# Reordering the rounding, the x sums and the direct sums in the second stage of a fused attention and leaky-ReLU feed-forward kernel

## The chip, the cores and the metric

The kernel runs on one core of a Trainium2 chip. The metric is the device time of one execution in microseconds (us). Engines go by the profile's names: PE multiplies matrices, PEld loads its weights, DVE is the vector engine, ACT the scalar engine, POOL is GpSimd, SP issues most of the transfers.

## The reference

```python
kv  = einsum('bhsd,bhse->bhde', k, v)          # 8 batches, 8 heads, 576 rows, 64 wide
out = einsum('bhsd,bhde->bhse', q, kv)
x   = out / sqrt(mean(out*out, -1) + 1e-6) * g_norm      # then (B,H,S,D) -> (4608, 512)
h   = x @ w_in                                 # 512 -> 2048
g   = maximum(0.01 * h, h)
y   = g @ w_out                                # 2048 -> 512, float32
```

`w_in` and `w_out` arrive in 64-bit floats and are rounded to 32-bit on the chip.

## The kernel before

**Stages.** The 4608 rows of x are cut into nine blocks of 512. Block 0 is multiplied directly while the weights are still arriving (`first_block`); the weights of the last quarter of the hidden width are not needed for it. After it come units of work, each one block by one quarter (chunk c) of the hidden width: block 1 with chunks 0 to 3 (units 0 to 3), block 0 with chunk 3 (unit 4), then blocks 2 to 8 with all chunks. Units 0 to 4 use one level of Strassen's seven products; from unit 5 on the first product uses two levels. This document calls units 0 to 4 the second stage.

**Slots.** A unit has seven slots, one for each product k of `ORDER = (1, 2, 6, 5, 7, 3, 4)`. The slot number is `at = 7 * now + t`, so unit 0 has slots 0 to 6, unit 1 slots 7 to 13, and so on to 34. A slot issues one product of h (eight matmuls into a bank named h_a to h_d) and, from slot 9 on, one product of the output of the unit before (into o_a or o_c): the o products run two slots behind. The bank of an h product has to be read by ACT or DVE before the product after the next can write it, and likewise o_a and o_c. In program order a slot then issues the postponed stores (`write_later`), the reads, a part of the rounding of a weight tile, the "direct" sums, and steps of the attention of block 2.

**Order.** `pin` keeps an instruction in program order. In the second stage all compute instructions are pinned, so each of PE, ACT, DVE, POOL and SP works through its own list, and an instruction that waits holds up what stands behind it. In `first_block` the sums made by `add` (L697) are not pinned.

**Rounding.** A tile's rounding (`round_f64`) has seven steps: two copies of its low and high words on ACT (L264, L262), a clamp on DVE (L266), an empty step, an activation on ACT (L271), and two instructions on DVE (L281, L284). There are 32 tiles. Tiles 0 to 23 are used by block 0; tile 22 and tile 23 are read by its last two output products. Tiles 24 to 31 are chunk 3. Tile j's raw words share a buffer with tile j + 2, so load j + 2 (`load_w`, SP) waits for tile j's two copies.

**x's sums.** `sides_x` makes the four sums of a block of x (DVE). For block 1 they are made near the end of `first_block`, by the letter x in `plan`.

**POOL.** L1198 is a copy of one element whose only purpose is a wait: POOL starts its sums behind it. Its list is then: `sides_w1(0)` and `more` (sums of the first weights, into `pairs`), `sides_w2` (also `pairs`), `combine(0, 0)`, and, slot by slot, the same for later chunks. At the end of every unit `sums_of` makes four sums gs1 to gs4 of g; output product 6 reads gs2, the third output product of the unit.

**combine and its homes.** `combine(c, part)` makes the second-level sums of chunk c into a home inside `stage` (six homes of 512 elements; a group of two products takes two homes, a group of one takes one), and postpones their store to a DRAM table. A home can be written again once the store has landed. Parts 0 and 1 come from `pairs`; part 2, the "direct" sums, comes from the weights themselves, in a first half (products 1 and 2) and a second half (product 4). Chunk 0's direct sums are on DVE, in slots 18 and 19 (first half), 22 and 23 (second half), both in home 2. The others are on POOL, by `DIRECT`.

```python
HOMES = {(0, 0): (2,), (0, 1): (4,), (1, 0): (0,), (1, 1): (2,), (2, 0): (4,), (2, 1): (0,),
         (3, 0): (4,), (3, 1): (0,), (0, 2): (2, 2), (1, 2): (2, 4), (2, 2): (0, 2), (3, 2): (4, 5)}
```

Of the kernel before, what the change touches and what calls it, by code (L numbers as in the profile page):

```python
# [24 lines left out]
def kernel(  # L25
# [36 lines left out]
    nc = tc.nc  # L62
# [29 lines left out]
    pin = tc.keep_in_program_order  # L92
    steady = first_done = in_line = in_first = in_block_1 = in_loop = False
# [13 lines left out]
    NW = U * NE * P  # L107
# [14 lines left out]
    def pair(i, *shape):  # L122
        return view(pairs, i * NW, *shape)
# [163 lines left out]
    w_jobs = []  # L287
# [7 lines left out]
    n0 = 4 * K * U  # L295
# [6 lines left out]
    def load_w(j, *eng):  # L302
        eng = eng or (nc.sync,)
        dst, src = w_jobs[j]
        if w_in.dtype == I64:
            w_raws[j] = load_f64(src.bitcast(U32), eng)
        else:
            load(dst, src, eng)

    def rounding(j, high_first=False):  # L310
        if w_in.dtype == I64:
            yield from round_f64(w_jobs[j][0], w_raws.pop(j), high_first)

    halfway = collections.deque()
# [15 lines left out]
    def finish_w():  # L330
        while halfway:
            for _ in halfway.popleft():
                pass
# [362 lines left out]

    def add(eng, out_, a, b_, minus=False, pinned=False):  # L697
        ins = eng.tensor_tensor(out_, a, b_, op=ALU.subtract if minus else ALU.add)  # L698
        if pinned or steady or in_block_1:
            pin(ins)  # L700

    def sides_w1(c):
# [16 lines left out]
    units = [(1, c) for c in range(NC)] + [(0, c) for c in range(K, NC)]  # L719
# [18 lines left out]
    def sides_w2(n):  # L738
# [7 lines left out]
        def sums(i):  # L746
# [15 lines left out]
            else:  # L762
# [13 lines left out]
    SLOT = {1: 0, 2: 1, 4: 2, 5: 3, 6: 4, 7: 5, 3: 6}  # L776
    w1_dram = [dram.tile([P, 7, 7, P], F32, name=f"w1_{c}") for c in range(NC)]
    HOMES = {(0, 0): (2,), (0, 1): (4,), (1, 0): (0,), (1, 1): (2,), (2, 0): (4,), (2, 1): (0,),
             (3, 0): (4,), (3, 1): (0,), (0, 2): (2, 2), (1, 2): (2, 4), (2, 2): (0, 2), (3, 2): (4, 5)}

    def combine(c, part, eng=None, only=(0, 1)):

# [315 lines left out]
                           pieces=pieces)  # L1098

    def go(steps, n=None):  # L1100
        while n is None or n > 0:
            if next(steps, steps) is steps:
                return
            n = None if n is None else n - 1
# [58 lines left out]
    t, a, f, x = "tafx"  # L1163
# [6 lines left out]
    loaded, x_sides = 12, None  # L1170
# [20 lines left out]
    in_first = True  # L1191
    first_block(between)
    in_first = False
    first_done = True
    rounded, rest = 26, collections.deque((3,))
    steps = halfway[0]
    in_block_1 = True
    pin(nc.gpsimd.tensor_copy(pair(0, NW)[:1, :1], x_sides[4][:1, 0, :1]))  # L1198
    h_sides, more = sides_w1(0)
    more()  # L1200
    sides_w2(0)[1](0)
    go(combine(0, 0))
    sides_w2(0)[1](1)
    in_loop = True

    LATE_ONE = {15: 2, 16: 2, 17: 1, 18: 1, 19: 2}
    A_SLOTS = {18: 1, 19: 2, 22: 1, 23: 1, 24: 2, 26: 1, 27: 1, 28: 2, 29: 2, 30: 1, 31: 1, 34: 2}
    DIRECT = {25: ((1, (0, 1)), (3, (1,))), 27: ((2, (0, 1)),), 29: ((3, (0,)),)}
    READS = {26: 2, 28: 4, 30: RING}
    PARTS = {33: ("11", "12"), 35: ("22",), 37: ("21",)}  # L1210

# [12 lines left out]
    def second_of(n):  # L1224
        if n in seconds:
            os_, finish = seconds.pop(n)
            return Second(n, os_["11"], finish)
# [7 lines left out]
    now, N1 = -1, NC + NC - K  # L1235
    rounds = [(1, range(NC)), (0, range(K, NC))] + [(i, range(NC)) for i in range(2, NB)]
    for i, chunks in rounds:
        one = in_block_1 = i < 2
        steady = not one
        if i == 1:  # L1240
            late, a_steps = a_steps, attention(2)
        elif i > 1:
            late, a_steps = a_steps, attention(i + 1, fine=True) if i + 1 < B else iter(())
        os = {}
        for c in chunks:
            now += 1
            nxt = units[now + 1] if now + 1 < len(units) else (NB, 0)
            g_sides = {}
            h_steps = product_h(now, h_sides, x_sides, g_sides) if one else \
                product_h_two(i, c, now, quarters, g_sides, second_of(now - 2))  # L1250
            for t in range(7):
                slot = 7 * c + t
                go(h_steps, 1)
                if not one:

                    if t == 6:
                        go(h_steps, 1)
                    if slot in LATE_SLOTS:
                        go(late, 1)
                    for _ in range(FINE_SLOTS.get(slot, 0)):  # L1260
                        go(a_steps, 1)
                    if i + 1 < NB:
                        if slot == 20:
                            x_sides, new_quarters, sums, inner = sides_x(i + 1)
                        if slot in (20, 21, 22):
                            go(sums, 2 if slot == 20 else 1)
                        if slot == 24:
                            inner(0)
                        elif slot == 25:
                            inner(1)  # L1270
                    load_some()

                if now - 1 in seconds:
                    for half in range(2):
                        if t == (6 if half else 4):
                            inner_g(now - 1, half)
                    if t == 5 and now - 1 < 2 * NC + NC - K:
                        inner_w2(units[now - 1][1])
                if (7 * now + t == 7 * NC + 4):
                    while writes:  # L1280
                        pin(nc.sync.dma_start(*writes.pop()))
                if slot in HELD and i == NB - 1:
                    pass
                elif waited == LAG:
                    go_o()
                elif o_queue:
                    waited += 1
                write_later()
                at = 7 * now + t
                for key in PARTS.get(at, ()):  # L1290
                    if at == 33:
                        part_os = os
                    load_part(part_os, key)
                if at in READS:
                    read(READS[at])
                if one:
                    if not rest and rounded < len(w_jobs):
                        finish_w()
                        steps = rounding(rounded)
                        rest.extend((3, 4) if rounded == 26 else (3, 3, 1))  # L1300
                        rounded += 1
                    if rest:
                        go(steps, rest.popleft())
                    if loaded < min(rounded + 2, len(w_jobs)):
                        load_w(loaded)
                        loaded += 1
                    for chunk, only in DIRECT.get(at, ()):
                        go(combine(chunk, 2, only=only))
                    if at == 18:
                        direct_0 = combine(0, 2, nc.vector)  # L1310
                    if at in (18, 19, 22, 23):
                        go(direct_0, 1)
                    if t == 3 and nxt[0] < 2 and nxt[1] != c:
                        h_sides, more_h = sides_w1(nxt[1])
                        if now == 0:
                            go(combine(0, 1))
                    if t == 5 and nxt[0] < 2 and nxt[1] != c:
                        more_h()
                    if t == 0 and units[now - 1][1] != c and now > 0:
                        for part in range(2):  # L1320
                            go(combine(c, part))
                    if at in (15, 16):
                        load_pair(2, at - 15)
                    go(late, LATE_ONE.get(at, 0))
                    go(a_steps, A_SLOTS.get(at, 0))
                    load_some(2 if at in (19, 20, 24, 25) else 1)
                    if at == 7 * NC - 4:
                        x_sides, _, sums, _ = sides_x(0)
                    elif at == 7 * N1 - 4:
                        x_sides, new_quarters, sums, inner = sides_x(2)  # L1330
                    if at in (7 * NC - 4, 7 * NC - 3, 7 * N1 - 4, 7 * N1 - 3):
                        go(sums, 2)
                    if at == 7 * N1 - 3:
                        inner(0)
                    elif at == 7 * N1 - 2:
                        inner(1)

            for _ in range(2 if i == NB - 1 and c == NC - 1 else 0):
                go(h_steps, 1)
                go_o()  # L1340
            go(h_steps)
            if c == NC - 1 and i != 1 and i + 1 < NB:
                inner(2)
                quarters = new_quarters
            by_two = NC + NC - K <= now < len(units) - 2
            if by_two:
                seconds[now] = (os, store(i))
            o_queue.append(product_o(now, g_sides, os, store(i), by_two))
# [32 lines left out]
```

## Time and profile before

| what | value |
|---|---|
| median of 3 runs (917.18 to 919.55) | 917.3 us |
| the profiled execution, its own time | 917.92 us |
| its span | 916.1 us |
| PE busy | 906.5 us (99%) |
| PEld, DVE, ACT, POOL busy | 783.6, 622.0, 346.9, 391.3 us |
| second stage, 112.9 to 228.5 us: busy of PE, DVE, ACT, POOL | 113.2, 78.1, 41.2, 101.0 us |
| granted clock of PE | 1.00 |
| transfers | 202.16 MB, mean 221 GB/s |

The profiled execution took 1.8 us more than its span, and 0.6 us more than the median. PE's share of busy time says that PE is nearly always at work; what it does not say is how tightly its products follow each other, since the end of a matmul is modelled. For that the starts are compared: eight matmuls of 128x256 start 1.73 us after the eight before them where nothing is late.

### The profile page before, as it was taken

What the parts mean: (1) busy time and instruction counts of PE and PEld (TensorE: products, weight loads), DVE (VectorE), ACT (ScalarE), POOL (GpSimd) and SP (SyncE); (2) the same over time, 40 slices, a digit from 0 to 9 for tenths busy, and PEclk for the clock granted to TensorE, in tenths of its full rate; (3) what the DMA queues carried; (4) which work ended last, traced back from release to release, by engine and by line L of the source; (5) the groups of instructions that cost most, each with busy time, mean ns of one, the idle gap of its engine ahead of it and who ended that gap; (6) DMA issues with size and microseconds to landing.
All of it is one profiled execution on the core that took longest, in us unless ns stands there. A gap on an engine that the chain in (4) does not pass through costs nothing.

```text
span 916.1 us, 18138 instructions
## 1 busy us (share of the span) xinstructions
PE 906.5 (99%) x7024; PEld 783.6 (86%) x7024; DVE 622.0 (68%) x1127; ACT 346.9 (38%) x679; POOL 391.3 (43%) x467
## 2 busy tenths in 40 slices
PE   8999999999999999999999999999999999999998
PEld 4544488878998999899999999999999999999997
DVE  5765865768657876587756786678659755755565
ACT  5756564221335233533343324332443333223330
POOL 2000499959633473226321642264226422642222
PEclk9999999999999999999999999999999999999999
DMA  8997185796998778876886789657765676667633
GB/s 257 256 249 198 55 274 170 234 325 199 348 329 264 228 212 267 234 228 217 249 264 218 220 249 272 222 174 230 223 183 178 188 221 198 181 189 225 195 111 93
DMA packets 92405, 202.16 MB, mean 221 GB/s; under 512 B 10016, under 2 KB 44448, under 8 KB 92320
## 3 DMA queue, kind: packets, MB, share of 16 engines
q1 hardware_dynamic: 81344, 189.14, 69.4%
q10 hardware_dynamic: 10528, 10.69, 3.4%
q8 instruction: 56, 0.92, 0.4%
q0 software_dynamic: 448, 1.18, 0.3%
q14 instruction: 29, 0.24, 0.1%
HBM read 173.44 MB, written 27.53 MB: 219 GB/s over the span
## 4 chain that ended last, share of the span: by engine, by line
PE 83%; DMA 6%; DVE 6%; ACT 3%; issue 1%; POOL 0%; SPq 0%; ACTq 0%; DVEq 0%; POOLq 0%
PE o_c L126 19%; PE o_a L126 19%; PE h_ha L126 11%; PE h_hb L126 11%; PE h_hc L126 8%; PE h_hd L126 8%; PE o_ps L126 3%; DMA pairs<-in_moe_w_out_dram 2%; PE h_b L126 1%; DMA stage<-in_moe_w_in_dram 1%; PE h_a L126 1%; DMA pairs<-in_v_dram 1%; PE h_c L126 1%; PE h_d L126 1%; DMA stage<-in_moe_w_out_dram 1%
## 5 line engine op out<-in xcount | busy, mean ns | idle before, releaser
L698 POOL TENSOR_TENSOR gs<-g 128x512 f32<-128x512 f32 x66 | 85.2, 1291 | 249.5 <-ACT g L913 249.5
L913 ACT ACTIVATE g<-g 128x512 f32<-128x512 f32 x127 | 80.1, 631 | 152.0 <-DVE g L698 150.1
L1032 ACT COPY w_all<-h_ha 128x512 f32<-128x512 f32 x84 | 48.9, 582 | 169.7 <-PE h_ha L126 159.6
L126 PE MATMUL o_a<-pairs,gs 128*128 128x256 f32 x392 | 93.1, 380 | 0.9 <-DVE o L698 0.9
L126 PE MATMUL o_c<-pairs,gs 128*128 128x256 f32 x392 | 93.3, 381 | 0.5 <-POOL gs L698 0.5
L698 DVE TENSOR_TENSOR o<-h_hb,o 128x128 f32<-128x128 f32 x104 | 29.9, 287 | 83.1 <-ACT pairs L1032 83.0
L126 PEld LDWEIGHTS o_c<-pairs,gs 128*128 128x128 f32 x392 | 71.3, 190 | 10.2 <-POOL pairs L698 1.2
L126 PEld LDWEIGHTS o_a<-pairs,gs 128*128 128x128 f32 x392 | 71.3, 190 | 9.2 <-issue 1.2
L698 DVE TENSOR_TENSOR o<-o_a,o 128x512 f32<-128x512 f32 (+1 forms) x93 | 62.6, 673 | 21.8 <-PE o_a L126 21.3
L698 DVE TENSOR_TENSOR o<-o_c,o 128x512 f32<-128x512 f32 x80 | 54.8, 684 | 26.4 <-PE o_c L126 26.2
L126 PE MATMUL h_ha<-stage,w_all 128*128 128x128 f32 x448 | 59.6, 276 | 0.0
L126 PEld LDWEIGHTS h_ha<-stage,w_all 128*128 128x128 f32 x448 | 56.6, 192 | 3.0 <-issue 0.7
L698 DVE TENSOR_TENSOR g<-g,pairs 128x512 f32<-128x512 f32 x84 | 55.7, 689 | 1.9
L698 POOL TENSOR_TENSOR pairs<-g 128x128 f32<-128x128 f32 x52 | 23.8, 457 | 77.2 <-PE h_hb L126 48.4
L698 DVE TENSOR_TENSOR w_all<-h_hc,w_all 128x512 f32<-128x512 f32 x56 | 38.4, 685 | 15.7 <-PE h_hc L126 15.6
L698 DVE TENSOR_TENSOR o<-h_hd,o 128x128 f32<-128x128 f32 x78 | 22.2, 285 | 38.1 <-ACT pairs L1032 38.0
L126 PE MATMUL h_hb<-stage,w_all 128*128 128x128 f32 x336 | 46.7, 275 | 0.0
L698 POOL TENSOR_TENSOR gs<-g,gs 128x512 f32<-128x512 f32 x33 | 45.5, 1380 | 0.0
L698 POOL TENSOR_TENSOR gs<-gs,g 128x512 f32<-128x512 f32 x33 | 44.1, 1335 | 2.6
L1032 ACT COPY pairs<-h_hb 128x384 f32<-128x384 f32 x84 | 40.0, 476 | 13.3 <-PE h_hb L126 12.6
L126 PE MATMUL o_acc<-w,g 128*128 128x512 f32 x96 | 43.7, 598 | 0.4 <-DVE w L284 0.3
L126 PE MATMUL h_ha<-xT,w_all 128*128 128x128 f32 x224 | 43.3, 275 | 0.2 <-ACT g L913 0.2
(240 smaller groups left out, 2242.3 us busy)
## 6 DMA issues: line engine op xcount, KB each, us to landing
w_all<-w SPq DMA_DIRECT2D x196, 448.0 KB, 4.2
pairs<-w SPq DMA_DIRECT2D x56, 512.0 KB, 4.4
out_dram<-o ACTq DMA_DIRECT2D x35, 256.0 KB, 5.2
v_in<-in_v_dram SPq DMA_DIRECT2D x27, 288.0 KB, 4.5
k_in<-in_k_dram SPq DMA_DIRECT2D x26, 288.0 KB, 4.1
q_in<-in_q_dram SPq DMA_DIRECT2D x52, 144.0 KB, 5.7
q_in<-in_q_dram SPq DMA_DIRECT2D x52, 140.0 KB, 5.7
w<-stage SPq DMA_DIRECT2D x12, 512.0 KB, 4.2
```

The source lines that it names most:

```text
L126: pin(nc.tensor.matmul(*args, **kw))
L698: ins = eng.tensor_tensor(out_, a, b_, op=ALU.subtract if minus else ALU.add)
L913: first_turn(nc.scalar.activation(t, t if src is None else src, func=AF.Prelu, alpha=SLOPE))
L1032: nc.scalar.copy(q[:, at], bank)
```

## The change

- `add` in `first_block` is pinned, so x's four sums for block 1 stand on DVE where the program has them: behind tile 22's rounding and ahead of tile 23's clamp.
- L1198, POOL's first instruction, reads tile 23's rounded weights in place of the last of x's sums.
- The rounding of tiles 25 to 31 follows a table. Its steps stay in their slots, but the two copies on ACT (and the load of the tile three ahead, on SP) are issued at the head of the slot, ahead of the slot's h product, where they were behind it.
- Chunk 0's second direct half goes from home 2 to home 5, and from slots 22 and 23 to slot 20 (both of its steps).
- Chunk 3's second direct half, in home 5, goes from POOL (slot 25) to DVE (slots 25 and 26).
- `combine(3, 0)` and `combine(3, 1)`, POOL, go from slot 21 to slot 22; their places in other units stay.

```diff
@@ def add
-        if pinned or steady or in_block_1:
+        if pinned or steady or in_first or in_block_1:
@@ HOMES
-             (3, 0): (4,), (3, 1): (0,), (0, 2): (2, 2), (1, 2): (2, 4), (2, 2): (0, 2), (3, 2): (4, 5)}
+             (3, 0): (4,), (3, 1): (0,), (0, 2): (2, 5), (1, 2): (2, 4), (2, 2): (0, 2), (3, 2): (4, 5)}
@@ after first_block
-    rounded, rest = 26, collections.deque((3,))
-    steps = halfway[0]
+    tiles = {25: halfway.popleft(), **{j: rounding(j) for j in range(26, len(w_jobs))}}
+    ROUND = {0: ((), ((25, 3),)), 1: (((26, 2),), ((25, 1), (26, 1))), 2: ((), ((26, 4),))}
+    for j in range(27, len(w_jobs)):
+        at = 3 * (j - 26)
+        ROUND.update({at: (((j, 2),), ((j, 1),)), at + 1: ((), ((j, 3),)), at + 2: ((), ((j, 1),))})
-    pin(nc.gpsimd.tensor_copy(pair(0, NW)[:1, :1], x_sides[4][:1, 0, :1]))
+    pin(nc.gpsimd.tensor_copy(pair(0, NW)[:1, :1], w_jobs[n0 - 1][0][:1, 0, :1]))
-    DIRECT = {25: ((1, (0, 1)), (3, (1,))), 27: ((2, (0, 1)),), 29: ((3, (0,)),)}
+    DIRECT = {25: ((1, (0, 1)),), 27: ((2, (0, 1)),), 29: ((3, (0,)),)}
@@ the slot, ahead of its h product
+                if one:
+                    for j, steps in ROUND.get(7 * now + t, ((), ()))[0]:
+                        go(tiles[j], steps)
+                        if loaded < min(j + 3, len(w_jobs)):
+                            load_w(loaded)
+                            loaded += 1
@@ the slot, behind it
-                    if not rest and rounded < len(w_jobs):
-                        finish_w()
-                        steps = rounding(rounded)
-                        rest.extend((3, 4) if rounded == 26 else (3, 3, 1))
-                        rounded += 1
-                    if rest:
-                        go(steps, rest.popleft())
-                    if loaded < min(rounded + 2, len(w_jobs)):
-                        load_w(loaded)
-                        loaded += 1
+                    for j, steps in ROUND.get(at, ((), ()))[1]:
+                        go(tiles[j], steps)
...
-                    if at == 18:
-                        direct_0 = combine(0, 2, nc.vector)
-                    if at in (18, 19, 22, 23):
-                        go(direct_0, 1)
+                    if at in (18, 25):
+                        direct = combine(*((0, 2, nc.vector) if at == 18 else (3, 2, nc.vector, (1,))))
+                    go(direct if at >= 18 else (), {18: 1, 19: 1, 20: 2, 25: 1, 26: 1}.get(at, 0))
...
-                    if t == 0 and units[now - 1][1] != c and now > 0:
+                    if t == now // 3 and units[now - 1][1] != c and now > 0:
                         for part in range(2):
                             go(combine(c, part))
```

More of the change, by code (lines that the diff above doesn't have):

```diff
@@ L1100, in go @@
     def go(steps, n=None):
+        steps = iter(steps)
         while n is None or n > 0:
```

## Prediction

> **What bounds the kernel.** The page first: PE is busy 99% of the span, so the time falls only by what PE waits, and rises by any new wait. Next, the view of waits for PE alone: engine and product, what released it, us in total, times, longest.
>
> ```profile
> PE o_a L126 <- DVE o L698: 0.9, 1, 0.9
> PE o_c L126 <- POOL gs L698: 0.5, 1, 0.5
> PE h_b L126 <- ACT g L938: 0.4, 1, 0.4
> PE h_a L126 <- issue: 0.3, 1, 0.3
> PE o_acc L126 <- DVE w L284: 0.3, 1, 0.3
> ```
>
> All five lie between 105 and 219 us; after 235 us the timeline of PE shows none. Modelled ends hide part of each, so I take starts from PE's timeline (start, duration):
>
> ```profile
> 105.42 3.67 PE L126 MATMUL o_acc<-w,g 128*128 128x512 f32 x8
> 109.38 3.67 PE L126 MATMUL o_acc<-w,g 128*128 128x512 f32 x8 [0.29 <-DVE w L284]
> ...
> 118.07 1.93 PE L126 MATMUL h_c<-xt,pairs 128*128 128x256 f32 x8
> 120.33 1.97 PE L126 MATMUL h_a<-xT,pairs 128*128 128x256 f32 x8 [0.33 <-issue]
> ...
> 188.77 1.99 PE L126 MATMUL h_b<-xT,pairs 128*128 128x256 f32 x8
> 191.64 1.97 PE L126 MATMUL o_a<-pairs,gs 128*128 128x256 f32 x8 [0.88 <-DVE o L698]
> ```
>
> Against 3.43 us (512 columns) and 1.73 us (256), the losses are: A, before the last two o_acc products, 0.28 + 0.53 = 0.8 us (tiles 22 and 23 late); B, slots 3 to 9, 0.53 + 0.07 + 0.21 + 0.10 + 0.58 + 0.07 = 1.5 us (ACT late at h's banks); C, slot 25, 2.87 − 1.83 (the usual step behind a kv group) + 0.07 = 1.1 us; D, slot 32 (2.35 − 1.73 + 0.10) and before slot 35 (0.3), 1.0 us. **Sum 4.4 us**, the most that can be won.
>
> C's cause is on DVE: chunk 0's second half waits for home 2's store, and the add that frees o_a stands behind it:
>
> ```profile
> 187.19 1.34 DVE L698 TENSOR_TENSOR stage<-w_all 128x128 f32<-128x128 f32 x1 [5.73 <-DMA w<-stage]
> 188.56 1.24 DVE L698 TENSOR_TENSOR stage<-stage,w_all 128x128 f32<-128x128 f32 x1
> ...
> 190.82 0.68 DVE L698 TENSOR_TENSOR o<-o_a,o 128x512 f32<-128x512 f32 x1
> ```
>
> **What the Trainium skill says.** "SBUF — State Buffer", SBUF: two separate sides, says that GpSimd and DVE share one port pair, an exclusive lock for a whole instruction, taken also by a DVE instruction with two SBUF inputs. The trace agrees: the two DVE adds above of 1.34 and 1.24 us overlap POOL sums, the same adds at 191.42 and 191.61, with POOL idle, take 0.26 and 0.27. "Perfetto Trace Analysis", Identifying the Most-Contended Engine, says that matmul busy time is a poor measure; the losses above, twice the waits listed, agree. "DMA: Bandwidth & Descriptors", Anatomy of one DMA, puts most of a transfer's fixed cost into the receipt of the last byte, so a home is free well after its store is issued: here the two stage stores at 187.35 take 3.4 and 4.4 us to land.
>
> **Part 1, x's sums and the gate.** Before, the sums fill DVE's gaps within tile 22 (starts 100.27 to 103.98). Behind it, from the same rows: the last multiply at 100.27 (1.0 us to the next start), clamp 101.27, L281 1.12 us after the clamp, L284 0.60 later, 102.99; four sums at 0.60: 103.60 to 106.0; tile 23's clamp 106.0, L281 107.12, L284 107.72, end 108.41. Tile 22 ends at 103.7 for 105.27: A's first loss goes. Tile 23 ends at 108.4 for 109.23, for POOL no longer runs beside it. The relu ahead of the last product then decides: it is 1.67 us behind L271 in ACT's list (105.64 to 107.31), so 108.12 to 108.7. A gains 0.8 − 0.2 = 0.6.
>
> The price is POOL's start. Its gate, now at 104.89, comes at 108.6: **3.8 us later**, with everything behind it. This is the list before:
>
> ```profile
> 104.89 0.75 POOL L1198 COPY pairs<-xt 1x1 f32<-1x1 f32 x1 [98.50 <-DVE xt L698]
> ...
> 123.02 1.53 POOL L698 TENSOR_TENSOR pairs<-w_all 128x512 f32<-128x512 f32 x1 [1.23 <-DMA w<-pairs]
> ...
> 134.62 1.28 POOL L698 TENSOR_TENSOR gs<-gs,g 128x512 f32<-128x512 f32 x1
> ```
>
> gs2 ends at 135.90; PE's third o product, slot 11, reads it at 138.65: 2.65 us of slack with 0.1 of latency. The wait of 1.23 us at 123.02 (a store of `pairs`) vanishes in the lateness, leaving 2.6. Contention may add 0.3 (the rounding now runs wholly beside POOL) or take up to 1.1 (tile 23 and the clamp of 24 are past). I take 2.2, ends 1.5 and 2.9. SP's store at 121.81 waits for POOL too, and load 29 (122.98) and the next `pairs` stores (125.72) wait behind it. I price that at nothing: load 29 is issued about 126, lands in 3 to 5 us, and slot 9's ACT then still has some 3 us before slot 11 needs its bank.
>
> **Part 2, copies at the head.** In slots 1, 3, 6, 9, 12 and 15 two ACT copies (start to start 0.57, 1.15 us a pair) go ahead of the bank's reader. In slot 1 they fall into ACT's wait of 1.90 us before 117.98, so slot 2's copy starts at its product's end and the 0.53 goes; clamp 27 comes earlier, which pulls slot 4's and 5's adds and the relus forward, and slot 7's copy ends about 0.3 us before slot 9 needs it. B's 1.5 us goes, counted alone; low end 0.9, should clamp and relus stay late.
>
> **A and B together** let PE reach slot 11 by 0.6 + 1.5 = 2.1 us earlier, but gs2 allows only 2.65 − 2.2 = **0.45** (−0.25 to 1.15). The rest becomes a wait on POOL at slot 11.
>
> **Part 3, direct sums.** Chunk 0's second half at slot 20 needs home 5, last stored in slot 17: free. Its four adds run beside POOL's 512-wide sums, up to 1.3 us each, from 176.9 to at most 182; the o_a add behind them must be done by 181.8. Cost 0 to 0.9, I take 0.4. C yields 1.1 − 0.4 = 0.7.
>
> Chunk 3's second half, now on DVE in slot 25, writes home 5 again. `combine(3, 0)` filled homes 4 and 5, now in slot 22 behind two 512-wide sums (2.5 us): POOL finishes it at 184.25 + 2.5 + 2.2 = 189. Its store belongs to slot 25 of SP, behind chunk 0's three stores, four `pairs` stores, one more, and six loads; at 0.5 to 0.8 us an issue after 183.8 that is about 191.7. It lands 3.4 us on, 195.1. DVE reaches the add at 192.8, so **DVE waits 2.3 us for a stage store once more**. Behind it on DVE stand two of x's sums and slot 26's h_d add; behind that add on ACT stand the relu and the four reads of o_ps (198.31 to 200.64, 2.33 us); behind those PE's next o_ps group, in slot 27:
>
> ```profile
> 201.45 0.88 PE L126 MATMUL o_ps<-qT,kv 64*32 64x384 f32 x16
> ```
>
> Landing + 0.4 + 2.3 (two short adds and two sums beside POOL) + 0.72 (add to relu) + 2.33 + 0.1 = landing + 5.9 = 201.0. PE would be there, with A to C won, at 201.45 − 1.15 = 200.3. So 0.7 us of the 1.15 goes back: **0.45 left** at slot 27 (from −1.0, landing at 196.5, to 1.15).
>
> POOL loses four 128-wide sums (1.8 us), and its wait of 11.15 us at 200.81, which stood on chunk 0's second half, ends. gs2 of unit 3 comes about 207 for 218.46: D's 0.7 goes; x's sums at 219 to 226 us, 1.2 to 1.8 us each beside POOL, fall back towards 0.6, so the 0.3 before slot 35 goes too. **D gains 1.0.**
>
> **Sum.** 0.45 + 1.0 = 1.45, taken as **1.5 us** (0 to 2.8 from the ends above). The profiled span of 916.1 us becomes 914.6, its execution 917.92 becomes 916.4; against the median, 0.6 us below that execution, 917.3 becomes 915.8. Beyond 235 us PE has no wait to absorb anything.
>
> **The rivals.**
> - *All gaps close.* POOL beside less DVE work is only 1.5 us late or less, and home 5's store lands by 194. For it: PE had 2.65 us of slack at slot 11. Against it: the 3.8 us. Won 3.7 to 4.4, so 913.3. Chance 0.17.
> - *Slower: home 5's store is late.* SP reached slot 25's stores only at 194.4 to 196.3 before. If it is as late again, the landing is about 199.7, PE's o_ps group starts at 205.6, 4.2 later than before, less D's 1.0: 920.5. Each us of landing counts fully; the result is slower than before from a landing at 196.6 and beyond the bound from 199.3. Against it: SP then stood behind a q load that waited for the DVE transpose at 189.73, itself behind the stall that goes. Chance 0.15.
> - *Slower, by the output's store.* SP's store at 219.38 had waited 11.0 us, put down to out_dram, a transfer that ACT issues in slot 31. If in the new order that wait falls ahead of the home 2 store of slot 27, POOL's next direct half and gs2 of unit 3 come behind it, at about 224: PE waits some 8 us in slot 32, 924. Chance 0.07.
> - *No effect.* The sums' order and the gate change little and the DVE wait only moves from slot 22 to 25: 917.3. Chance 0.05.
>
> **How the numbers follow.** About 0.3% (2.75 us) is what a measurement can tell from no change. The forecast has 0.56: nearly all of it inside, 0.03 beyond on the fast side. Faster: 0.17 + 0.03 = 0.20. Slower: 0.15 + 0.07 = 0.22. Same: 0.53 + 0.05 = 0.58. The forecast's own range is 914.5 to 917.3; the range goes to 913.4 (all gaps closed, nearly) and to 921.0 (home 5 late), leaving out the out_dram case and the ends.
>
> **What would show it.** POOL's L1198 at 108 to 109 us; the o_acc products 3.4 and 3.4 to 3.7 apart; no ACT wait of PE in slots 4 and 9, but one on POOL gs (or `pairs`) by slot 11, at 137.5 to 139; no DVE wait at 181 to 187, but one of 1 to 4 us on w<-stage near 193; o_ps in slot 27 near 201; no POOL wait of PE at slot 32. It is wrong if slot 11 starts before 137 (POOL kept up), if the DVE wait is absent, or if PE waits anywhere after 230 us.

## The result, and the profile after

The changed kernel takes **921.74 us** (median of 10, 920.84 to 922.99) beside 917.59 us for the kernel before (10 runs, 916.77 to 921.07). The ratio is 1.0040, 95% interval 1.0029 to 1.0052: slower, where 915.8 had been forecast. The profiled execution has a span of 919.3 us (916.1 before) and took 921.13 us, 0.6 us under its median.

The waits of PE come first again (engine and product, what released it, us in total, times, longest):

```profile
PE o_ps L126 <- ACT xT L421: 3.2, 1, 3.2
...
PE h_a L126 <- DVE g L698: 0.6, 1, 0.6
PE h_c L126 <- POOL stage L698: 0.6, 1, 0.6
...
PE h_b L126 <- ACT g L938: 0.3, 1, 0.3
PE o_acc L126 <- ACT g L1144: 0.3, 1, 0.3
```

The waits of o_a on DVE (0.9) and of o_c on POOL (0.5) are gone. In their place stands one of 3.2 us that before did not have, and two of 0.6 at h's banks. PE's timeline after (start, duration) shows where:

```profile
104.77 3.60 PE L126 MATMUL o_acc<-w,g 128*128 128x512 f32 x8
108.66 3.70 PE L126 MATMUL o_acc<-w,g 128*128 128x512 f32 x8 [0.29 <-ACT g L1144]
...
117.42 1.99 PE L126 MATMUL h_c<-xt,pairs 128*128 128x256 f32 x8
119.25 1.89 PE L126 MATMUL h_a<-xT,pairs 128*128 128x256 f32 x8
121.73 1.97 PE L126 MATMUL h_c<-xT,pairs 128*128 128x256 f32 x8 [0.59 <-POOL stage L698]
124.34 1.99 PE L126 MATMUL h_a<-xt,w_all 128*128 128x256 f32 x8 [0.64 <-DVE g L698]
...
190.75 1.89 PE L126 MATMUL o_a<-pairs,gs 128*128 128x256 f32 x8
...
203.76 2.00 PE L126 MATMUL o_ps<-qT,kv 64*32 64x384 f32 x16 [3.21 <-ACT xT L421]
205.69 2.79 PE L126 MATMUL h_a<-xT,w_all 128*128 128x256 f32 x8
```

Differences of such starts cut the time into stretches, which every kernel below is compared by. "h" is the last product of h in block 0 (101.71 before, 101.34 after), "11" the o_a product of slot 11, "25" that of slot 25, "27" the o_ps group of slot 27, "35" the first h_ha product, "end" PE's last matmul. All in us:

| kernel | h to 11 | 11 to 25 | 25 to 27 | 27 to 35 | 35 to end |
|---|---|---|---|---|---|
| before | 36.94 | 52.99 | 9.81 | 27.02 | 684.35 |
| after | 37.46 | 51.95 | 13.01 | 27.91 | 684.35 |
| after less before | +0.52 | -1.04 | +3.20 | +0.89 | 0.00 |

The sum is +3.57; h's earlier start takes off 0.37, which leaves the 3.2 us between the spans. So most of the loss lies in slots 25 to 32, and nothing moves behind slot 35.

**Slot 27.** The chain runs back from the o_ps group to ACT's reads, to DVE's add of h_d, to a wait of DVE, to SP's list. ACT, DVE and SP after, in their timelines:

```profile
201.85 0.63 ACT L913 ACTIVATE g<-g 128x512 f32<-128x512 f32 x1 [9.23 <-DVE g L698]
202.39 0.85 ACT L415 ACTIVATE sum<-o_ps 128x384 f32<-128x384 f32 x2
203.13 1.05 ACT L421 ACTIVATE xT<-o_ps,g_sb 128x384 f32<-128x384 f32 x2
```

```profile
198.41 0.55 DVE L698 TENSOR_TENSOR stage<-w_all 128x128 f32<-128x128 f32 x1 [5.05 <-DMA w<-stage]
...
201.14 0.68 DVE L698 TENSOR_TENSOR g<-h_d,g 128x512 f32<-128x512 f32 x1
```

```profile
188.81 2.50 SPq L168 DMA_DIRECT2D q_in<-in_q_dram  x4
191.41 1.37 SPq L138 DMA_DIRECT2D k_in<-in_k_dram  x1
192.83 0.43 SPq L138 DMA_DIRECT2D v_in<-in_v_dram  x1
193.36 1.17 SPq L735 DMA_DIRECT2D w<-stage  x2
```

Home 5's store is issued at 193.36, behind six loads that hold SP for 4.5 us (1.3 us of them, in the load of k, the view of waits puts down to a product of PE); POOL had finished the sums at 190.8. It lands at 198.29, 4.93 us on. DVE, which had nothing to do from 193.4, starts chunk 3's add 0.1 us later, and what stands behind it follows in order until PE starts at 203.76.

**The clock.** The next lines are the view of windows: window, its length, then busy us and instructions of PE, PEld, DVE, ACT and POOL, the clock granted to PE, the share of the DMA engines that is busy, GB/s.

```profile
203.00:204.00 1.00, 0.24 (x1) 0.14 (x2) 1.00 (x2) 1.00 (x3) 1.00 (x2) 0.96 1.08 399
204.00:205.00 1.00, 1.00 (x16) 0.22 (x14) 0.48 (x1) 0.67 (x2) 0.92 (x2) 0.50 0.96 382
205.00:206.00 1.00, 1.00 (x16) 0.31 (x2) 0.00 (x0) 0.15 (x1) 1.00 (x3) 0.50 1.10 344
206.00:207.00 1.00, 1.00 (x3) 0.82 (x3) 0.62 (x2) 1.00 (x3) 0.64 (x1) 0.50 1.12 375
207.00:208.00 1.00, 1.00 (x5) 0.83 (x5) 0.52 (x2) 0.66 (x2) 0.00 (x0) 0.83 1.09 366
```

After its pause PE works at half clock for 3.4 us. The o_ps group and the h_a product behind it take 203.76 to 208.32, 4.56 us; before they took 2.63. That is another **1.93 us**, so the fourth stretch is 1.93 lost and 1.04 won. Not all of it is the clock. The group's first matmul starts at 203.76 and its second only at 204.23, 0.47 us later, when ACT's second read (L421, to 204.18) is done. e5 and e14 below have the same 0.47 us at full clock, and e5 takes 3.10 us for the whole. So **1.46 us** are the clock's and 0.47 still ACT's lateness. Nine of the ten executions have a mean clock of 0.998 or 0.996, which is what 3.4 us or more at half clock make of 919, so it is no accident of the profiled one; the tenth, at 1.00, took 921.03 us, within the range of the others.

### The profile page after: what moved, and what is told of

It is laid out like the page before. It is cut to its first block, busy times and chain, and to the rows that moved or that the text cites. A ratio compares the mean times of both kernels' runs of the same rounds, so it can differ in the third digit from the quotient of the medians.

```text
span 919.3 us, 18146 instructions
## 1 busy us (share of the span) xinstructions
PE 908.2 (99%) x7024; PEld 784.8 (85%) x7024; DVE 622.0 (68%) x1131; ACT 346.6 (38%) x679; POOL 388.1 (42%) x463
## 4 chain that ended last, share of the span: by engine, by line
PE 90%; DVE 4%; ACT 2%; DMA 2%; issue 1%; POOL 1%; ACTq 0%; DVEq 0%; POOLq 0%
PE o_c L126 19%; PE o_a L126 18%; PE h_ha L126 11%; PE h_hb L126 10%; PE h_hc L126 8%; PE h_hd L126 8%; PE h_ps L126 3%; PE o_acc L126 3%; PE o_ps L126 3%; PE h_a L126 2%; PE h_c L126 1%; DMA pairs<-in_v_dram 1%; PE h_b L126 1%; DMA w<-stage 1%; PE kv_ps L126 1%
```

## The experiments

Every ratio is to the kernel before on the same chip, with its 95% interval. The diffs are against the kernel after unless another is named. The stretches of all of them, as above, from one profile each:

| run | h to 11 | 11 to 25 | 25 to 27 | 27 to 35 | 35 to end | median, us |
|---|---|---|---|---|---|---|
| e1 | 37.47 | 51.95 | 9.73 | 25.99 | 685.57 | 917.97 |
| e2 | 37.47 | 51.95 | 9.73 | 26.12 | 684.54 | 916.50 |
| e9 | 37.46 | 51.95 | 9.73 | 25.99 | 689.11 | 920.46 |
| e14 | 36.64 | 51.95 | 9.78 | 26.46 | 684.34 | 916.96 |
| e5 | 37.47 | 51.95 | 13.89 | 26.46 | 684.34 | 919.51 |
| e3 | 38.04 | 51.95 | 9.73 | 25.99 | 685.81 | 918.16 |
| e4 | 39.97 | 52.47 | 9.73 | 25.99 | 685.85 | 920.69 |
| e8 | 38.06 | 52.37 | 9.73 | 25.99 | 685.57 | 918.28 |
| e10 | 37.12 | 52.07 | 9.73 | 26.02 | 687.58 | 919.64 |
| e11 | 37.48 | 51.95 | 9.73 | 25.99 | 684.34 | 916.22 |
| e12 | 37.14 | 52.08 | 9.73 | 25.99 | 684.34 | 915.93 |
| e13 | 36.02 | 51.96 | 9.81 | 30.36 | 684.35 | 917.55 |

One profile is no fine measure of the first two stretches. Up to slot 25 no edit separates before, e13 and e14, and they take 36.94, 36.02 and 36.64 us, then 52.99, 51.96 and 51.95.

### Is it chunk 3's half on DVE? (e1, e2)

```diff
-    DIRECT = {25: ((1, (0, 1)),), ...
+    DIRECT = {25: ((1, (0, 1)), (3, (1,))), ...      # e1: back on POOL, nothing on DVE in 25, 26
-    if at in (18, 25):                               # e2: on DVE, two slots later
+    if at in (18, 27):
...
-    {18: 1, 19: 1, 20: 2, 25: 1, 26: 1}
+    {18: 1, 19: 1, 20: 2, 27: 1, 28: 1}
```

> The changed kernel with chunk 3's second direct half back on POOL in slot 25; all else as changed. Theory (DVE's wait of 5.0 us for home 5's store holds the relu and the o_ps reads behind it, PE stands 3.3 us in slot 27 and then runs 3.4 us at half clock, 1.9 us more): both go, 921.7 - 5.2 = 916.5 us (915.5 to 917.5), no PE wait on ACT xT in slot 27, clock 1.0 throughout. Rival (the loss lies in the first slots, POOL's late start, and everything in slot 27 is late anyway): 919.5 us or more, and a wait of 2 us or more at slot 27 remains.

> The changed kernel with chunk 3's second direct half still on DVE, but in slots 27 and 28 in place of 25 and 26. Theory (the wait for the store is what costs, not the engine): home 5 is free by then, 916.5 us (915.5 to 917.5), no DVE wait over 1 us on w<-stage. Rival (DVE is the wrong engine, its sums are drawn out beside POOL): 918 us or more, with new PE waits on DVE in slots 28 to 30.

e1: 917.97 us for 916.5 expected, ratio 1.0004 (0.9996 to 1.0012). e2: 916.50 us, as expected, 0.9989 (0.9982 to 0.9996). In e2 the store of home 5 comes behind POOL's next writing of it, so part of the computation is changed: product 4's sums of chunk 3 carry other numbers, and its time is not that of a kernel that does the same work. In both, slot 27's 3.2 us and the half clock are gone, so DVE's place in slots 25 and 26 is where they came from. e1 doesn't get all of it: behind slot 35 it loses 1.22 us (685.57 for 684.35), where PE waits 0.9 us for POOL. POOL had waited 4.7 us there for a stage store, and SP had stood still for 11.0 us before it. That was not expected. e9 has the same stop of SP and shows where it comes from; no run here takes it away from e1.

### The place alone, with the sums as they were (e9)

```diff
-    if at in (18, 25):
+    if at in (18, 27):
...
-    {18: 1, 19: 1, 20: 2, 25: 1, 26: 1}
+    {18: 1, 19: 1, 20: 2, 27: 2}
```

> The kernel after, with both DVE steps of chunk 3's second half in slot 27 (after had them in slots 25 and 26). Theory (the loss in slot 27 is DVE standing behind home 5's store, landed at about 198): DVE's add comes after the landing, o_ps in slot 27 starts near 201 with no wait of 3 us and no half clock; the loss of 3.2 + 1.9 us goes, 916.5 us, ratio to the kernel before 0.9990. Rival (DVE's two adds late in the unit hold back the eviction of o or h there): some 0.5 to 1.5 us lost in slots 28 to 30, 917.0 to 918.0. Prediction's parts 1 and 2 right after all would show as 915.8.

920.46 us, ratio 1.0024 (0.9994 to 1.0053): the forecast of 916.5 was wrong, and its rival was too. Up to slot 35 all went as the theory said: 25 to 27 in 9.73 and 27 to 35 in 25.99. Then 4.76 us were lost at once. PE's line, POOL's, and SP's waits between 200 and 230 us in e9:

```profile
236.27 1.65 PE L126 MATMUL h_ha<-stage,w_all 128*128 128x128 f32 x6 [2.49 <-POOL stage L698]
```

```profile
230.33 0.72 POOL L698 TENSOR_TENSOR stage<-w_all 128x256 f32<-128x256 f32 x1 [8.94 <-DMA w<-stage]
```

```profile
SPq L735 <- DMA out_dram<-o: 12.0, 1, 12.0
```

POOL stands behind home 5's store, which DVE had ready at 204 us but SP issued only at 226.3, because SP had stood still from 206.3 to 218.3 on a transfer of **ACT's**: the first output store of the second stage, issued at 216.06. The trace's records give the reason: in this program each of these transfers signals one of eight semaphores, in turn over all queues, and SP's `pairs` store at 218.34 has the one of that output store, eight transfers back in the program's order. So SP doesn't go past the eighth transfer behind one that another engine issues late; e11 to e13 below test it. The prediction had this as its third rival, "by the output's store", at 0.07 and for slot 32; the mechanism exists, behind slot 35.

### Home 5 early, DVE as changed (e14)

```diff
-    DIRECT = {25: ((1, (0, 1)), (3, (1,))), ...        # against before
+    DIRECT = {25: ((1, (0, 1)),), ...
+                    if at == 25:
+                        direct_3 = combine(3, 2, nc.vector, (1,))
+                    if at in (25, 26):
+                        go(direct_3, 1)
```

> The kernel before with chunk 3's second half on DVE in slots 25 and 26 and nothing else. Home 5's stage store is issued at about 187.4 there (side sums of chunk 3 in slot 21), lands at about 191.7, and DVE reaches the add at about 193. Theory (the loss of after in slot 27 is the lateness of that store, not the two adds on DVE): no wait of DVE of over 0.5 us at 193, o_ps of slot 27 at 201.4, no half clock; POOL has 1.8 us less, and the time is 916.8 to 917.6. Rival (the adds on DVE in slot 25 themselves delay h's sum and the reads of o_ps): o_ps of slot 27 at 202 or later, 918.5 or more. Second rival (the store is late there too, as SP's list is what it was): DVE waits 2 us or more, 920.

916.96 us, ratio 0.9992 (0.9981 to 1.0003), as expected. The side sums of chunk 3 are still in slot 21 here, home 5's store goes out at 186.07, and DVE's add waits for nothing:

```profile
196.25 0.28 DVE L698 TENSOR_TENSOR stage<-w_all 128x128 f32<-128x128 f32 x1
```

25 to 27 takes 9.78. So what cost was the store that the adds waited for. In themselves the two adds cost half a us: the o_ps group starts in time, but its second matmul comes 0.47 us behind the first, when ACT's second read is done, and that is what 26.46 has above 25.99. 11 to 25 falls to 51.95 as well, though chunk 0's half still waits 5.8 us for home 2: its adds, at 187.46, took 0.29 and 0.70 us instead of 1.34 and 1.24.

### Is the half clock a cost of its own? (e5)

```diff
+                    if at == 27:
+                        idle = ps_m.tile([P, NT], F32, tag="ha", name="idle_ps")
+                        for _ in range(3):
+                            matmul(idle, lhsT=ident, rhs=w2_sb[0][3][:, 0, :], start=True, stop=True)
```

> The kernel after, with three matmuls of 128x512 put into slot 27 ahead of the o_ps group; their product is not read by anything. They take 3 x 0.86 us at full clock and lie in the 3.2 us in which TensorE waited for ACT's reads of o_ps. Theory (half clock is what the idle stretch starts): the granted clock stays near 1.0 from 204 to 207 us, the stretch from o_ps to the second h_a behind it falls from 4.56 to about 2.7 us, the o_ps start stays at 203.8, and the time goes from 921.7 to about 919.8. Rival (the low clock has another cause, such as a window of its own): clock still 0.5 in 204 to 207 us, time 921.7. Second rival (the added matmuls push the o_ps group): o_ps starts later than 204.2 and the time is 920.5 or more.

919.51 us, ratio 1.0021 (1.0011 to 1.0030); after had 1.0040. Two windows of e5, in the same columns:

```profile
205.00:206.00 1.00, 1.00 (x16) 0.30 (x16) 0.70 (x2) 0.89 (x2) 0.92 (x2) 1.00 1.02 400
206.00:207.00 1.00, 1.00 (x12) 0.68 (x4) 0.05 (x1) 0.57 (x2) 1.00 (x2) 1.00 1.09 346
```

The clock stays at 1.00, and from o_ps to the start of the product behind h_a it takes 3.10 us (204.99 to 208.09) for 4.56. The forecast had about 2.7; the difference is the 0.47 us that the group's second matmul waits for ACT. PE's lines:

```profile
204.99 1.34 PE L126 MATMUL o_ps<-qT,kv 64*32 64x384 f32 x16 [1.52 <-ACT xT L421]
206.26 1.99 PE L126 MATMUL h_a<-xT,w_all 128*128 128x256 f32 x8
```

In the profiled execution DVE waited 5.9 us for the store instead of 5.0, so o_ps starts 1.2 us later than expected; PE still waited 1.5 us for ACT behind the added matmuls, so they did not push it. The medians differ by 2.2 us for the 1.9 expected. In e4, e9 and e10, where some executions have the half clock and some don't, those with a mean clock of 1.00 are the fastest: in e10 918.70 to 919.19 us, the others 919.57 to 922.15.

### Parts 1 and 2 by themselves (e3, e4, e8)

All three have chunk 3's half on POOL, as e1 has. e3 puts the gate back on x's last sum, e4 puts the copies and loads back behind the h product (the load in question is that of the tile two ahead, not three), e8 does both; x's sums stay in order in all.

```diff
-    pin(nc.gpsimd.tensor_copy(pair(0, NW)[:1, :1], w_jobs[n0 - 1][0][:1, 0, :1]))
+    pin(nc.gpsimd.tensor_copy(pair(0, NW)[:1, :1], x_sides[4][:1, 0, :1]))      # e3, e8
...
-                    for j, steps in ROUND.get(7 * now + t, ((), ()))[0]:        # e4, e8: from the head
-                        go(tiles[j], steps)                                     # of the slot, load_w too,
...
+                    for j, steps in ROUND.get(at, ((), ()))[0]:                 # to behind its h product
+                        go(tiles[j], steps)
```

> As e1_chunk3_pool, with POOL's first instruction reading the last of x's sums again. Theory (the gate at tile 23 moves the contention of POOL and DVE onto tiles 26 and 27, which makes slots 5 and 6 late): POOL starts at 106.2 us in place of 108.6, slots 4 to 9 lose 0.5 to 1 us less, the last two products of block 0 up to 0.4 more: 0.3 us faster than e1 (-0.8 to +0.2). Rival (the gate is what saves block 0's last products): 0.4 us or more slower than e1.

> As e1_chunk3_pool, with the two ACT copies of tiles 26 to 31 (and their loads) behind the slot's h product again. Theory (the copies at the head of slot 3 hold back the read of h_c that slot 5 needs, 0.75 us, and save about 0.5 us at slot 4): between 0.4 us faster and 0.3 us slower than e1. Rival (as the prediction had it, the copies at the head win 1.5 us): 1 us or more slower than e1.

> The kernel after with chunk 3's second half on GpSimd in slot 25, GpSimd's gate on x's last sum as before, and copies and loads behind the h product as before; x's sums in order behind tile 22 stay. Beside it stand the kernels with the late gate and copies at the head (918.0), early gate and copies at the head (918.2), late gate and copies behind (920.7). Theory (the copies at the head only repair what the late gate spoils): about 918, at most 0.5 from the second. Rival (the copies at the head are worth the same under both gates): 920.5 to 921. In both cases the wait of 1.8 us ahead of the last o_acc product stays, as it comes with the gate on x's last sum and the sums in order.

| | copies at the head | copies behind |
|---|---|---|
| gate on tile 23 | e1: 917.97, h to 11 37.47 | e4: 920.69, 39.97 |
| gate on x's last sum | e3: 918.16, 38.04 | e8: 918.28, 38.06 |

Ratios: e3 1.0001 (0.9990 to 1.0013), e4 1.0032 (1.0020 to 1.0045), e8 1.0006 (0.9998 to 1.0015). Two expectations fell; e8 came as expected, with the copies at the head worth 0.1 us under the early gate. e3 was to gain 0.3 us on e1 and did not: with the sums in order and POOL let in early, tile 23's rounding runs beside POOL, and the last product of block 0 waits. e4 was to change little and lost 2.7, which its rival had (1 us or more): DVE's add for h_a comes too late in slot 6, and the product behind that pause takes 3.26 us (125.95 to 129.21) for 1.83, at half clock. PE's waits in e3, then in e4:

```profile
PE o_acc L126 <- DVE w L284: 1.8, 1, 1.8
```

```profile
PE h_a L126 <- DVE g L698: 2.3, 1, 2.3
```

The late gate is thus a cure for what the ordering of the sums does to tile 23, and the copies at the head are a cure for what the late gate does to slots 5 to 7. Together they bring the stretch to 37.46 in after and to 37.46 to 37.48 in e1, e2, e5, e9 and e11, the five others with all of parts 1 and 2. Without them it is 36.94 in before and 37.12, 37.14, 36.02 and 36.64 in e10, e12, e13 and e14. On average that is 36.77: **parts 1 and 2 cost some 0.7 us** of profiled time, 0.3 to 1.4 against the single profiles. The kernels that differ in these parts alone, e11 and e12, are 0.34 us apart in this stretch and 0.29 us in their medians, which the noise could make. e8, which of the edits of parts 1 and 2 has only the sums in order, stands at 38.06, 1.3 above that average: the ordering is what costs, and gate and heads win part of it back. The late gate was not tried with the sums unordered.

### The direct sums alone, and SP's stop taken away (e10 to e13)

e10 is the kernel before with part 3 alone, chunk 3's half on DVE in slot 27. e11 is e9, e12 is e10 and e13 is the kernel before, each with this edit, which lets SP issue that one output store in its own order:

```diff
+            here = i == 1 and key == "11"
-            nc.scalar.dma_start(
+            ins = (nc.sync if here else nc.scalar).dma_start(
...
+            if here:
+                pin(ins)
```

> The kernel before with the direct sums of the change alone (chunk 0's second half in home 5, its add in slot 20; chunk 3's and 0's side sums in slot 22; chunk 3's second half on DVE, in slot 27); x's sums, GpSimd's gate and the copies as before. Theory (parts 1 and 2 together lose 0.5 us, part 3 gains 1.0 at slot 25 and 1.0 by slot 35 once its store has landed): slot 11 is where it was before, 917.5 - 2.0 = 915.5, some 0.5 to 1.0 us below the kernel with the same direct sums and parts 1 and 2. Rival (the prediction's, parts 1 and 2 together gain 0.45): 0.5 us above that kernel. Second rival (the gains of part 3 need POOL late or the copies early): 917 or more.

> The kernel after with chunk 3's second half on DVE in slot 27, and the first 512 KB-quadrant store of the output (o11 of the second tile) issued by SP in its own order instead of by ACT. The same without the second edit ran in 920.5 us: it won 5.3 us by slot 35 against after and lost 3.6 us at the h_ha product behind it, where POOL stood 8.9 us behind a stage store; SP had stood still from 206.3 to 218.3 us on a `pairs` store that follows that output store by eight transfers. Theory (SP can't issue a transfer while the eighth one before it in the planner's order, of whatever queue, has not landed; ACT issues that output store late): SP has no stop of 12 us, POOL waits at most 3 us there, no wait of PE on h_ha and no half clock; slot 35 stays near 226.4; time 920.5 - 1.5 (POOL's wait for PE 2.5 with 1.6 of half clock, less 0.9 of pipelining kept) at the least and 916.0 at the best, I take 916.0. Rival (POOL stands behind the stage store because SP had too much to issue): POOL's wait and h_ha's stay, 920.5.

> The kernel before with the direct sums of the change (chunk 3's second half on DVE in slot 27) and that output store on SP. Without the second edit it ran in 919.6 us, with slot 35 at 226.1. Theory as for the kernel above: no stop of SP, no wait at h_ha, 915.7, some 0.3 below the kernel with the late gate and copies at the head, since its slot 35 was 0.3 earlier. Rival (parts 1 and 2 gain when nothing is in the way): 0.5 above it. Second rival (the wait at h_ha comes from SP's load): 919.6.

> The kernel before with that output store on SP and nothing else. In before SP stood still from 207.8 to 219.4 us and POOL's unit-3 sums were late at slot 32 (0.7 us of PE) and x's sums slow before slot 35 (0.3). Theory (those came from the transfer order): SP's stop goes; POOL is released earlier only if its wait of 11.15 us to 212 hung on this, which the trace puts on a store issued at 196 to 204 us, so most likely only what follows slot 32 moves: 917.0 to 917.6. The prediction's step D (the loss stood on chunk 0's second half, not on SP's stop): 917.5. Rival (D is SP's stop): slot 35 at 227.5 and 916.5.

e10: 919.64 us, ratio 1.0027 (1.0017 to 1.0036), for 915.5 expected. It lost 3.23 us behind slot 35 in the same way as e9 (SP still for 10.6 us, POOL for 7.8). e11: 916.22 us, 0.9983 (0.9974 to 0.9992). e12: **915.93 us, 0.9981 (0.9972 to 0.9990)**, the lowest median of this study. Both are within 0.3 us of what was expected. In both the last stretch is back at 684.34; POOL in e11 goes through where it had stood for 8.9 us:

```profile
222.74 0.73 POOL L698 TENSOR_TENSOR stage<-stage,w_all 128x256 f32<-128x256 f32 x1
223.43 1.18 POOL L698 TENSOR_TENSOR stage<-w_all 128x256 f32<-128x256 f32 x1
```

One edit at one transfer takes 4.2 us off e9 and 3.7 off e10, so SP's stop is shown to be the cause there. e13: 917.55 us, 0.9997 (0.9987 to 1.0007), no change, as expected: taking away the stop of 11.0 us gains nothing in the kernel before, where the loss at slot 32 had been put down to chunk 0's second half. e12 and e13 differ in part 3 alone, with chunk 3's half in slot 27: with the store on SP it is worth 1.6 us. (e13's profiled execution, at 918.56 us, has a late gs sum at slot 32 and half clock behind it, hence the 30.36; its 13 other runs show a mean clock of 1.0.)

## Why the prediction was wrong

- **Slot 27, the term that failed.** The prediction had the place, the chain and the wait, and sized them too small: home 5's store issued at 191.7, plus 3.4 to land, plus 5.9 to the o_ps group, 201.0. Measured: 193.36 + 4.93 + 5.47 = 203.76. DVE waited 5.05 us, not 2.3, and the loss was 3.2 us for 0.7. The issue is 1.7 us of it. From 183.87 to 193.36 SP issued 13 transfers, 0.73 us each; that lies within the 0.5 to 0.8 us that the prediction allowed, but 191.7 has 14 of them at 0.56. The flight, from issue to landing, is 1.5 us of it. The transfers' view for 186 to 200 us gives the two stage stores of that stretch

```profile
w<-stage SPq DMA_DIRECT2D x2, 512.0 KB, 5.2
```

  a median of 5.2 us, while the prediction took 3.4, the shorter of the two flights it had quoted (the other was 4.4). So it took the cheap end of both ranges where every us of landing counted. Why this flight was longer stays open: the DMA engines were as busy in before (share 1.05 from 188 to 192 us, the flights of 3.4 and 4.4) as in after (0.85 from 192 to 194, 1.02 from 194 to 198.3). The section on one DMA that the prediction cites describes a transfer issued by GpSimd; these are SP's, and their lengths here are measured.
- **The rival was the case.** "Home 5's store is late", 0.15, was right in kind. It gave 920.5 us with a landing at 199.7; the landing was 198.29, for which its own rule gives 919.1. That 920.5 lies near the 921.74 measured is thus in part luck: the rest is the clock, and what A and B did not win.
- **The clock was missing.** A pause of PE was priced at its own length, the clock behind it at nothing. "TensorE: Matmul & The Clock Gate", Part 1: The HAM clock gate, says that an idle window of about 3.4 us halves the clock and a busy one restores it. The 3.4 us for which the half clock lasted agree. The pause of 3.2 us was shorter than that window and halved the clock all the same. The rival's pause (205.6 less 200.3 us) was longer than the page's window, so this was in reach: half of 3.4 us, an estimate of 1.7 us from the page's figure, for the 1.46 measured.
- **A: half right at most.** Tile 23 ended at 108.41 (108.4 forecast), the gate came at 108.64 (108.6) and the last o_acc product at 108.66 (108.1 to 108.7). h to slot 0 took 10.85 us for 11.18, 0.33 won instead of 0.6. But e10, e12 and e13, which have the first block as it was before, take 10.79 to 10.80, and e14 11.07, so a gain from the edit is not shown.
- **B: wrong.** Its 1.5 us (the six terms add up to 1.56) did not go; slot 0 to slot 11 grew from 25.76 to 26.60. Slot 2's 0.53 went as argued, and the copies that gained it moved on: in slot 3 ACT has L271 and tile 27's two copies ahead of h_c's read, and DVE's clamp, on which the next add waits, takes 1.49 us beside POOL for 0.43 before. ACT, then DVE, after:

```profile
119.35 0.63 ACT L271 ACTIVATE w<-cut 128x512 int32<-128x512 f32 x1 [0.84 <-DVE cut L266]
119.89 0.66 ACT L264 ACTIVATE add<-early 128x512 uint32<-128x512 uint32 x1
120.45 0.67 ACT L262 ACTIVATE cut<-early 128x512 f32<-128x512 f32 x1
121.02 0.57 ACT L940 COPY g<-h_c 128x512 f32<-128x512 f32 x1
```

```profile
122.20 1.49 DVE L266 TENSOR_SCALAR cut<-cut 128x512 f32<-128x512 f32 x1
123.61 0.68 DVE L698 TENSOR_TENSOR g<-h_a,g 128x512 f32<-128x512 f32 x1
```

  The first ends at 121.59 and PE starts slot 5 at 121.73; the second at 124.29 and slot 6 at 124.34. (The waits above put slot 5 down to a stage sum of POOL. That sum ended at 121.73, and PE had begun to load slot 5's weights at 121.70.) The clamp's length hangs on who is first. In before it starts at 122.99, 0.03 us ahead of POOL's sum, and takes 0.43 us. In e10, which has neither gate nor heads, POOL's sum starts at 122.02 and the clamp at 122.05; it takes 1.52 us, and PE waits 1.1 us in slot 6 there too.

  The limit that had been named, gs2 at slot 11, never came to bear: gs2 ended at 138.10, 2.2 us later as forecast, for a product at 138.79, since nothing had been won ahead of it. A and B together were -0.52 for +0.45.
- **C: the number came, its cause is not shown.** 1.04 us for 0.7; the four adds in slot 20 cost nothing. But e13 and e14 leave chunk 0's half in home 2 and in slots 22 and 23, DVE waits 6.2 and 5.8 us for the store there, and they take 51.96 and 51.95 us as well. e13:

```profile
185.98 0.38 DVE L698 TENSOR_TENSOR stage<-w_all 128x128 f32<-128x128 f32 x1 [6.20 <-DMA w<-stage]
186.40 0.70 DVE L698 TENSOR_TENSOR stage<-stage,w_all 128x128 f32<-128x128 f32 x1
```

  The same adds took 1.34 and 1.24 us in before, so the old order does not lose C's 1.1 us in every execution.
- **D: right**, 27.02 to 25.99 in e1, e9 and e11 (26.02 in e10), 1.03 for 1.0. It needs only one of its two reasons: e1 has chunk 3's sums on POOL, e14 has POOL's wait to 200.60, and PE waits for POOL in slot 32 in neither.
- **The sum.** -0.52 + 1.04 - 3.20 - 1.93 + 1.04 = -3.57, where +1.5 had been written. Of the gains, D was there for its reason, C in number only, A and B not; the change lost by one wait and what the wait set off.

## What to carry to other kernels

Before moving a write into a buffer that is still to be stored, price the store as SP's queue at that moment (what stands ahead, at its own measured lengths) plus a flight, and take the worse end of both if something else waits for it. Count a pause of PE of some 2.3 us or more as the pause and, possibly, 1.5 to 1.7 us for the clock. Before pricing a loss that one profile shows, look whether a second profile of the same order has it. And when a kernel has transfers on several queues with completion semaphores given out in turn, look for stops of one queue on another's late transfer: here they cost nothing until an earlier part was made faster, and then they took the gain.

## What was not expected of the hardware

Half clock came after pauses shorter than 3.2 us too, and not each time. e9's h_ha pause of 2.49 us was followed by a clock of 0.50 for the next windows, and e13's of 2.42 us at slot 32 and e4's of 2.27 in slot 6 likewise; each time the half clock lasted about 3.4 us and cost 1.5 to 1.7 us. Pauses of 1.52 us (e5) and 1.78 us (e3, e8) were followed by full clock, and so was e9's h_ha pause in e10, again 2.49 us long:

```profile
236.07 0.94 PE L126 MATMUL h_ha<-stage,w_all 128*128 128x128 f32 x6 [2.49 <-POOL stage L698]
```

The six matmuls took 0.94 us there and 1.65 in e9. The page named above says that the window runs freely, so that a pause could count or not by where it falls; but it asks for an idle window of about 3.4 us, and these pauses are shorter. Here the measurement decides: 2.27 us can be enough. No run here shows where the window lies or how much of it has to be idle.
